# A planner whose lock between VectorE's and GpSimd's copies is more exact and covers Q copies too

## The chip, the cores and the metric

One core of a Trainium2 chip. The rounds of the experiments ran on three different chips, each with the kernel before alongside (714.64, 714.82 and 714.95 us). The metric is the device time of one execution in microseconds (us). The profile describes one execution; its span (first to last instruction) is 1.5 to 2.2 us shorter than the time in the runs on record. The granted TensorE clock was 1.00, within 0.003, in every profiled run here.

## The reference, cut to what matters

```python
def reference(A_x, A_wqkv, A_wo, B_x, B_w_gate, B_w_up, B_w_down, gate_w):   # S=2048, D=512
    x = A_x
    g = sigmoid((x * gate_w).sum(-1, keepdims=True))
    # a: 32 heads of width 16, softmax(q k^T / 4) v, then @ wo
    # b: ((x @ w_gate) * (x @ w_up)) @ w_down, inner width 1376
    return g * a + (1 - g) * b
```

Most of the time (693 of 713 us of the span, below) goes to the exponentials of the attention: 32 heads x 2048 x 2048 scores. In tiles of 128 keys x 512 queries that is 32 x 16 x 4 = 2048 score tiles. The kernel takes them in 32 rounds ("heads" in the prediction), each of four heads and one block of 512 queries, so 64 tiles.

## The kernel before

The kernel's Python simulates the five engines with a table of durations, picks at each step what an engine does next, and so fixes the order of all instructions on every engine. Only that order and the semaphores reach the chip. Three kinds of work matter here. (PSUM and SBUF are the two on-chip memories in which the kernel places its tiles. psS, psX and psO, which TensorE's matmuls write here (`PE MATMUL psS<-QM,KE` on the page), are allocated in PSUM, and the kernel calls 512 columns of them a bank; the other tiles are in SBUF.)

- ScalarE turns two or three score tiles at a time from PSUM into probabilities (1524 of the 2048 tiles).
- VectorE evaluates the other 524 by an integer trick (an "eviction" from PSUM), and then VectorE or GpSimd make three shifted copies of each pair of tiles, SBUF to SBUF ("probability copies").
- When the queries of a head block change, VectorE makes two masked copies of Q, SBUF to SBUF as well ("Q copies"). TensorE needs them for the next scores.

An extract, with comments added; `...` stands for lines left out:

```python
        # f_q: after the projection, PSUM -> qtmp, then two masked copies
        ev_q[c, b, p] = add("dve", [e0, o_mask] + q_last.get((c - 1, b), []),
            lambda v, p=p: v.tensor_scalar(QM[:, p, b, :], qtmp[:], mask[:, p : p + 1], None, ALU.mult),
            0.22, prio=3.2)
        ...
        # try_copy: one probability copy, on VectorE or on GpSimd
        if eng == "dve":
            fn = lambda v: v.tensor_single_scalar(cell_ap(c, I16), cell_ap(src, I16), 32.0 * k, ALU.add)
            occ = DCP + 0.133 * n           # 0.341 us for two tiles
        else:
            fn = lambda g: g.tensor_scalar(cell_ap(c, I16), cell_ap(src, I16), 32.0 * k, 1.0, ALU.add, ALU.mult)
            occ = PCP + 0.435 * n           # 1.01 us for two tiles
        ...
        # gen_step: the lock between VectorE's and GpSimd's copies
        if eng == "pool" and t < lock["dve"]:
            clock[eng] = lock["dve"]        # in the plan GpSimd waits for a VectorE copy to end
            return True
        ...
                if eng == "pool" or lock["pool"] <= t:   # VectorE copies wait for GpSimd
                    c = try_copy(eng, t)
        ...
        if eng == "pool":
            lock["pool"] = clock["pool"]
```

The planner's lock covers probability copies. A Q copy goes through the last lines of `gen_step` as an ordinary VectorE task: it neither waits for GpSimd nor holds it in the plan.

On the chip they do hold each other up, by the trace of this kernel. A Q copy that is not held takes 344 ns (mean of 20). Others, each begun while a GpSimd instruction ran, last 492 to 1169 ns and end 145 to 150 ns after it. 40 two-tile probability copies on VectorE (418 ns in the median where no GpSimd instruction overlaps them) also begin while one runs and end 277 to 282 ns after it. That is what "held" means below. Evictions from PSUM are not: 685.7 ns in the mean where a GpSimd instruction overlaps them (440), 682.7 where none does (84). The other way round, 33 GpSimd copies that begin 155 to 175 ns after a two-tile VectorE copy began take 1.152 us in the median, against 1.043 where no VectorE copy overlaps them. What on the chip makes the copies wait is not shown.

The softmax here doesn't subtract the row's maximum and nothing guards it: scores larger than these inputs give would overflow.

Of the kernel before, what the change touches and what calls it, by code (L numbers as in the profile page):

```python
# [13 lines left out]
class _Op:  # L14
# [5 lines left out]
    def __init__(self, eng, fn, deps, stream, inc):  # L20
        self.eng = eng
        self.fn = fn
        self.deps = deps
        self.stream = stream
        self.inc = inc
        self.seq = 0
        self.count = 0
        self.waits = []
        self.needed = False
        self.know = None  # L30
# [82 lines left out]

class _Task:

    __slots__ = ("eng", "deps", "fn", "occ", "lat", "prio", "cb", "stream", "dma", "op", "start", "end", "alloc", "pre")

    def __init__(self, eng, deps, fn, occ, lat=None, prio=5, cb=None, stream=None, dma=False, alloc=None):
        self.eng = eng
        self.deps = [d for d in deps if d is not None]  # L120
        self.fn = fn
        self.occ = occ
        self.lat = occ + 0.13 if lat is None else lat
        self.prio = prio
        self.cb = cb
        self.stream = stream
        self.dma = dma
        self.op = None
        self.start = None
        self.end = None  # L130
        self.alloc = alloc
        self.pre = None


class _Cell:

    __slots__ = ("need", "readers")
# [59 lines left out]
def _build(nc, A_x, A_wqkv, A_wo, W_gate, W_up, W_down, gate_w, out):  # L197
# [37 lines left out]
    with ExitStack() as stack:  # L235
# [243 lines left out]
            return old  # L479

        PACK = 0.2135
        PLAT = 0.44
        SW = 0.11
        pe = {"mode": "c"}
# [119 lines left out]
        def f_q(c, b, pos):  # L604
            packs = [
                (
                    lambda bk, kt=kt: col(
                        bk.ap, wq[:, kt, b * 128 : (b + 1) * 128], xT[:, kt, c * 512 : (c + 1) * 512], kt == 0, kt == KD - 1
                    ),
                    PACK,  # L610
                    "c",
                )
                for kt in range(KD)
            ]

            def evac(bk, last):
                if QT and (c or b):
                    bk.need += 1
                    e0 = add(
                        "dve",  # L620
                        [last] + qt_last,
                        lambda v: v.tensor_single_scalar(qtmp[:], bk.ap, QS, ALU.mult),
                        0.6,
                        prio=2,
                        cb=lambda k: bk.readers.append(k),
                    )
                    qt_last.clear()
                    for p in range(2):
                        ev_q[c, b, p] = add(
                            "dve",  # L630
                            [e0, o_mask] + q_last.get((c - 1, b), []),
                            lambda v, p=p: v.tensor_scalar(QM[:, p, b, :], qtmp[:], mask[:, p : p + 1], None, ALU.mult),
                            0.22,
                            prio=3.2,
                        )
                        qt_last.append(ev_q[c, b, p])
                    return
                bk.need += 2
                for p in range(2):
                    ev_q[c, b, p] = add(  # L640
                        "dve",
                        [last, o_mask] + q_last.get((c - 1, b), []),
                        lambda v, p=p: v.tensor_scalar(QM[:, p, b, :], bk.ap, mask[:, p : p + 1], QS, ALU.mult, ALU.mult),
                        0.66,
                        prio=2,
                        cb=lambda k: bk.readers.append(k),
                    )

            def deps():
                if c and not q_done.get((c - 1, b)):  # L650
                    return [None]
                return [d_wq[b]] + xdep(c)

            return Fill(f"q{c}{b}", packs, deps, evac, pos)
# [445 lines left out]
        def try_copy(eng, t):  # L1100
            best = None
            if eng == "pool" and dve_busy(t) < PB:
                return None
            for i, pr in enumerate(pairs):
                if not pr["k"] or not full(pr):
                    continue
                r = max(k.end for k in pr["p1"]) + (0.0 if eng == "dve" else SEM)
                if r > t:
                    continue
                if eng == "pool":  # L1110
                    k = pr["k"][-1]
                    if k < PK:
                        continue
                else:
                    k = pr["k"][0]
                    if k == 3 and r + (0.5 if st["ua"] >= NA - 12 else KW) > t:
                        continue
                best = (pr, k)
                break
            if best is None:  # L1120
                return None
            pr, k = best
            prs_ = [pr]
            if eng == "dve" and M4 and len(pr["u"]) == 2:
                for p2 in pairs[i + 1 : i + 4]:
                    if k in p2["k"] and full(p2) and len(p2["u"]) == 2 and max(x.end for x in p2["p1"]) <= t:
                        if even(pr["cell"] + p2["cell"]):
                            c = alloc(4, t)
                            if c is not None:
                                prs_.append(p2)  # L1130
                                break
            us = [(p_, x) for p_ in prs_ for x in range(len(p_["u"]))]
            n = len(us)
            c = alloc(max(n, 2), t)
            if c is None:
                return None
            c = c[:n]
            old = claim(c, 1)
            for p_ in prs_:
                p_["k"].remove(k)  # L1140
                if not p_["k"]:
                    pairs.remove(p_)
            if n == 4:
                _build.m4 += 1

            def cb(tk):
                for i, (p_, x) in enumerate(us):
                    cells[p_["cell"][x]].readers.append(tk)
                    add_tile(*p_["u"][x], k, c[i], tk)

            I16 = mybir.dt.int16
            src = tuple(p_["cell"][x] for p_, x in us)
            if eng == "dve":
                fn = lambda v: v.tensor_single_scalar(cell_ap(c, I16), cell_ap(src, I16), 32.0 * k, ALU.add)  # L1154
                occ = DCP + 0.133 * n
            else:
                fn = lambda g: g.tensor_scalar(cell_ap(c, I16), cell_ap(src, I16), 32.0 * k, 1.0, ALU.add, ALU.mult)  # L1157
                occ = PCP + 0.435 * n
            return _Task(eng, [x for p_ in prs_ for x in p_["p1"]] + old, fn, occ, cb=cb)
# [301 lines left out]
        PCP = 0.14  # L1461
        DEV = 0.6
        RSV = 0.5
        NP = 8
        KP = 1
        FBL = 15
# [233 lines left out]
        def gen_step(eng):  # L1700
            t = clock[eng]
            best = None
            if eng == "pool" and t < lock["dve"]:
                clock[eng] = lock["dve"]
                return True
            for k in qs[eng]:
                if best is not None and k.prio >= best.prio:
                    continue
                r = ready(k)
                if r is not None and r <= t:  # L1710
                    if k.alloc is not None:
                        old = k.alloc(t)
                        if old is None:
                            WHY.append((t, "p1cell"))
                            continue
                        k.deps = k.deps + old
                        k.alloc = None
                    best = k
# [4 lines left out]
            if eng in ("dve", "pool") and (best is None or best.prio > CPR):  # L1723
                if eng == "pool" or lock["pool"] <= t:
                    c = try_copy(eng, t)
                    if c is not None:
                        if eng == "dve":
                            lock["op"] = lock["prev"]
                            lock["prev"] = c
                        elif lock["op"] is not None:  # L1730
                            c.deps.append(lock["op"])
                        run_task(c, t)
                        lock[eng] = clock[eng]
                        return True
            if best is None:
                return False
# [1 line left out]
            if eng == "pool" and lock["op"] is not None:  # L1738
                best.deps.append(lock["op"])
            run_task(best, t)  # L1740
            if eng == "dve":
                lock["prev"] = best
            if eng == "pool":
                lock["pool"] = clock["pool"]
            return True

        o_woz = add(
# [208 lines left out]
```

## Time and profile before

| | before |
|---|---|
| time, median | 714.72 us (3 runs), 714.83 with a fourth run |
| span of the profile | 713.1 us |
| busy: ScalarE, TensorE, VectorE, GpSimd | 699.1, 688.0, 643.2, 439.2 us |
| exponentials on ScalarE | 496 of two tiles, 177 of three, 1 of one |
| Q copies | 30, mean 515 ns, longest 1169 ns |

How to read it: I split the span into four parts. The *lead* runs to the start of the first exponential, the *closing chain* from the end of the last one. Between them lie the exponentials. A *gap* is where the end of an exponential comes 0.04 us or more later after the end of the one before than is normal for its size (0.49, 0.917 and 1.344 us for one, two and three tiles). For before: lead 9.13, exponentials 693.03, gaps 1.47, closing 9.46, together 713.09 us. The gaps are worked out from the single instructions of the trace. They show waiting that the busy share hides, since ScalarE's records overlap (a two-tile one lasts 1.36 us in the median, while the ends lie 0.917 us apart).

### The profile page before, as it was taken

The page shows a single profiled execution, that of the slowest core. Times are in us where ns is not written, and L with a number is a line of the kernel's source. Part 1 is how long each engine was busy: PE and PEld are TensorE (multiplying, and loading weights), DVE is VectorE, ACT ScalarE, POOL GpSimd, SP SyncE. Part 2 cuts the span into 40 slices and gives each one's busy share as a digit, 9 for nine tenths or more (in the row PEclk, how much of TensorE's full clock was granted, in tenths as well). Part 3 has the DMA queues.
Part 4 walks back from the last instruction along what each step waited for, and adds up shares of the span by engine and source line. Part 5 has one row for each costly group of instructions (what it writes and reads, how often), then busy time and mean ns, then how long its engine had stood idle before and what let it go on. Part 6 is the DMA issues. An engine that isn't in the chain of part 4 may idle for free. (4 is left out here: it accounts for less than half of the span.)

```text
span 713.1 us, 21304 instructions
## 1 busy us (share of the span) xinstructions
PE 688.0 (96%) x9115; PEld 188.2 (26%) x9115; DVE 643.2 (90%) x1229; ACT 699.1 (98%) x689; POOL 439.2 (62%) x463
## 2 busy tenths in 40 slices
PE   8999999999999999999999999999999999999997
PEld 3323232222222222222222222222222222222222
DVE  5999989999999888899988888999889988999887
ACT  6999999999999999999999999999999999999995
POOL 4648676565656566576577566655557676555682
PEclk9999999999999999999999999999999999999999
DMA  7700001000200001000000010000000000000001
GB/s 142 255 12 9 21 18 19 19 17 22 81 20 18 17 16 32 26 17 17 20 3 28 17 44 25 18 13 10 21 18 17 18 28 29 17 21 18 3 20 46
DMA packets 33055, 21.65 MB, mean 30 GB/s; under 512 B 20381, under 2 KB 27965, under 8 KB 32961
## 3 DMA queue, kind: packets, MB, share of 16 engines
q1 hardware_dynamic: 31632, 19.64, 9.2%
q8 instruction: 71, 1.16, 0.7%
q10 hardware_dynamic: 1328, 0.66, 0.4%
q14 instruction: 24, 0.19, 0.1%
HBM read 15.12 MB, written 2.36 MB: 25 GB/s over the span
## 5 line engine op out<-in xcount | busy, mean ns | idle before, releaser
L1689 ACT ACTIVATE PT<-psS 128x1024 bf16<-128x1024 f32 (+1 forms) x577 | 625.9, 1420 | 0.7 <-PE psS L488 0.6
L1157 POOL TENSOR_SCALAR PT<-PT 128x1024 int16<-128x1024 int16 x220 | 237.0, 1086 | 146.1 <-DVE PT L1154 38.9
L488 PE MATMUL psS<-QM,KE 32*128 32x512 bf16 x1968 | 255.2, 376 | 12.3 <-ACT PT L1689 6.6
L1076 DVE TENSOR_SCALAR PT<-psS 128x512 int16<-128x512 f32 x328 | 221.8, 685 | 23.9 <-PE psS L488 20.2
L1219 PE MATMUL psO<-PT,VS 128*18 128x512 bf16 x1709 | 227.7, 381 | 0.7 <-DVE oraw L1248 0.6
L1219 PE MATMUL psO<-PT,VD 128*18 128x512 bf16 x1231 | 192.3, 381 | 0.1
L1017 PEld LDWEIGHTS <-KE 32*128 32x128 bf16 x2048 | 63.1, 91 | 279.4 <-issue 166.4
L1154 DVE TENSOR_SCALAR PT<-PT 128x1024 int16<-128x1024 int16 (+1 forms) x232 | 101.4, 466 | 2.1 <-PE psO L1219 0.8
L1157 POOL TENSOR_SCALAR PT<-wv 128x1024 int16<-128x1024 int16 x57 | 61.0, 1078 | 40.9 <-DVE wv L1076 16.5
L1219 PEld LDWEIGHTS psO<-PT,VS 128*18 128x18 bf16 x1709 | 52.2, 88 | 59.8 <-issue 42.4
L1689 ACT ACTIVATE wv<-psS 128x1024 bf16<-128x1024 f32 (+1 forms) x47 | 60.3, 1311 | 0.0
L557 PE MATMUL psX<-wd,hT 128*32 128x512 bf16 (+1 forms) x704 | 59.0, 386 | 0.3 <-DVE wk L867 0.3
L1076 DVE TENSOR_SCALAR wv<-psS 128x512 int16<-128x512 f32 x76 | 51.8, 686 | 6.8 <-PE psS L488 6.3
L1219 PEld LDWEIGHTS psO<-PT,VD 128*18 128x18 bf16 x1231 | 45.3, 88 | 36.4 <-issue 22.9
L557 PE MATMUL psX<-xT,wu 128*32 128x512 bf16 x688 | 53.2, 383 | 1.0 <-DVE wv L1076 0.7
L557 PE MATMUL psX<-xT,wg 128*32 128x512 bf16 x688 | 52.5, 383 | 1.0 <-DVE PT L1076 0.7
L1219 PE MATMUL psO<-wv,VS 128*18 128x512 bf16 x182 | 49.9, 381 | 0.5 <-DVE oraw L1248 0.5
L1076 DVE TENSOR_SCALAR PT<-psX 128x512 int16<-128x512 f32 x58 | 39.8, 686 | 6.6 <-PE psS L488 6.4
L1689 ACT ACTIVATE wd<-psS 128x1024 bf16<-128x1024 f32 (+1 forms) x35 | 42.0, 1289 | 0.0
L1219 PE MATMUL psO<-wv,VD 128*18 128x512 bf16 x167 | 38.2, 381 | 0.0
L1157 POOL TENSOR_SCALAR wv<-PT 128x1024 int16<-128x1024 int16 x24 | 25.6, 1068 | 20.3 <-PE psO L1219 10.0
L830 DVE TENSOR_TENSOR hT<-psX,usb 128x512 bf16<-128x512 f32 (+1 forms) x44 | 30.0, 682 | 4.4 <-PE psX L557 4.3
(127 smaller groups left out, 704.0 us busy)
## 6 DMA issues: line engine op xcount, KB each, us to landing
rb<-rscr SPq DMA_DIRECT2D x31, 256.0 KB
out_dram<-ost SPq DMA_DIRECT2D x12, 128.0 KB, 1.7
wu<-in_B_w_up_dram SPq DMA_DIRECT2D x1, 1376.0 KB, 10.1
wg<-in_B_w_gate_dram SPq DMA_DIRECT2D x1, 1376.0 KB, 13.0
wd<-in_B_w_down_dram SPq DMA_DIRECT2D x1, 1280.0 KB, 6.1
OT<-OX SPq DMA_DIRECT2D x60, 16.0 KB, 1.8
wo<-in_A_wo_dram SPq DMA_DIRECT2D x1, 512.0 KB, 13.0
out_dram<-wk SPq DMA_DIRECT2D x4, 128.0 KB, 1.7
```

The source lines that it names most:

```text
L488: return e.add_instruction(mybir.InstMatmult(name=nc.get_next_instruction_name(), engine=mybir.EngineType.PE, ins=[e.lower_ap(rhs), e.lowe ...
L557: return e.matmul(out_ap[32 * q : 32 * q + w, :], lhs[:, 32 * q : 32 * q + w], rhs, start=s0, stop=s1, tile_position=(0, 32 * q), skip_gro ...
L830: lambda v: v.tensor_tensor(hT[0:w, f, :], bk.ap[0:w, :], usb[0:w, n % 2, :], ALU.mult),
L1017: r = e.ldweights(w, tile_position=pos)
L1076: lambda v: v.tensor_scalar(cell_ap(pr["cell"][i : i + 1], mybir.dt.int16), bk.ap, CB, 0.0, ALU.add, ALU.max),
L1154: fn = lambda v: v.tensor_single_scalar(cell_ap(c, I16), cell_ap(src, I16), 32.0 * k, ALU.add)
L1157: fn = lambda g: g.tensor_scalar(cell_ap(c, I16), cell_ap(src, I16), 32.0 * k, 1.0, ALU.add, ALU.mult)
L1219: r = e.matmul(psO[32 * j : 32 * j + VW, :], pv_stationary(m, kt, j, k), cell_ap((cell,)), start=s0, stop=s1, tile_position=(0, 32 * j), s ...
L1689: lambda a: a.activation(cell_ap(c), src, ACT.Exp, scale=LN2 / 128.0),
```

## The change

Its intent: plan Q copies at 0.26 us (the trace has 256 to 264 ns from the start of one that is not held to the next instruction's start) and put them under the lock too; let each side start somewhat before the other's planned end (0.07 us before that of a VectorE copy, 0.1 us before that of a GpSimd copy); let GpSimd hold back when a Q copy is due within 0.3 us; and keep SBUF cells in reserve for the round that is accumulated now. The diff is cut to the lines that matter:

```diff
+        QMC = 0.26
+        LKD = -0.07
+        LKP = 0.1
+        QMP = 3.2
+        QMW = 0.3
@@ f_q
-                            0.22,
-                            prio=3.2,
+                            QMC,
+                            prio=QMP,
+                            x4=True,
@@ try_copy
-            c = alloc(max(n, 2), t)
+            c = alloc(max(n, 2), t, False, RSC * sum(len(x["k"]) for x in pairs if x["u"][0][0] <= pvst["m"]) if pr["u"][0][0] > pvst["m"] else 0)
@@ gen_step
-            if eng == "pool" and t < lock["dve"]:
-                clock[eng] = lock["dve"]
+            if eng == "pool" and t < lock["dve"] + LKD:
+                clock[eng] = lock["dve"] + LKD
+                return True
+            if eng == "pool" and QMW and clock["dve"] <= t + QMW and any(k.x4 and (ready(k) or 1e9) <= t + QMW for k in qs["dve"]):
+                clock[eng] += 0.05
                 return True
...
+                    if k.x4 and lock["pool"] > t:
+                        continue
...
-                        lock[eng] = clock[eng]
+                        lock[eng] = clock[eng] - (LKP if eng == "pool" else 0.0)
...
-            if eng == "dve":
+            if eng == "pool":
+                lock["pool"] = clock["pool"] - LKP
+            elif eng == "dve":
+                if best.x4:
+                    lock["dve"] = clock["dve"]
+                    lock["op"] = lock["prev"]
                 lock["prev"] = best
-            if eng == "pool":
-                lock["pool"] = clock["pool"]
```

`RSC` is 1.0. `lock["op"]` makes the next GpSimd instruction wait, by a real semaphore, for the VectorE instruction just ahead of the copy that is to go first.

More of the change, by code (lines that the diff above doesn't have):

```diff
@@ L114, with __init__ @@
 class _Task:
-    __slots__ = ("eng", "deps", "fn", "occ", "lat", "prio", "cb", "stream", "dma", "op", "start", "end", "alloc", "pre")
-    def __init__(self, eng, deps, fn, occ, lat=None, prio=5, cb=None, stream=None, dma=False, alloc=None):
+    __slots__ = ("eng", "deps", "fn", "occ", "lat", "prio", "cb", "stream", "dma", "op", "start", "end", "alloc", "pre", "x4")
+    def __init__(self, eng, deps, fn, occ, lat=None, prio=5, cb=None, stream=None, dma=False, alloc=None, x4=False):
         self.eng = eng
@@ L132, in __init__ @@
         self.pre = None
+        self.x4 = x4
 class _Cell:
@@ L1463, in _build @@
         RSV = 0.5
+        RSC = 1.0
         NP = 8
```

## The prediction

> **What bounds the kernel now.** The kernel's Python is a planner: it simulates the five engines with a small table of durations, decides the order of every instruction on each engine, and emits that fixed order with semaphores. So the change adds no work to the chip; it changes the order that the planner finds. I therefore first ask which engine has any time to give back.
>
> I read the busy rows, then the groups:
>
> ```profile
> PE 688.0 (96%) x9115; PEld 188.2 (26%) x9115; DVE 643.2 (90%) x1229; ACT 699.1 (98%) x689; POOL 439.2 (62%) x463
> ...
> L1689 ACT ACTIVATE PT<-psS 128x1024 bf16<-128x1024 f32 (+1 forms) x577 | 625.9, 1420 | 0.7 <-PE psS L488 0.6
> ...
> L632 DVE TENSOR_SCALAR QM<-qtmp,mask 128x512 bf16<-128x512 bf16 x30 | 14.3, 515 | 0.1
> ```
>
> ScalarE (ACT) is busy 699.1 of 713.1 us, and in the exponentials (L1689) it sits idle only 0.7 us before those that write PT. GpSimd (POOL) has 38% free and VectorE (DVE) 10%. The bound is ScalarE's exponentials. From the list of single instructions I take their rate: ends of neighbours lie 0.917 us apart where the second covers two score tiles (496 such), 1.344 us where it covers three (177), and one covers a single tile (about 0.49). 496 x 0.917 + 177 x 1.344 + 0.49 = 693.2 us; from the start of the first (9.1 us) to the end of the last (703.6 us) it is 694.5 us. The rest is 9.1 us of lead-in and 9.5 us of closing chain. Tiles: 2 x 496 + 3 x 177 + 1 = 1524, exactly the planner's own share for ScalarE (29 heads x 48 + 3 x 44), so no VectorE tile was shifted to ScalarE (`convert`) that a better plan could give back.
>
> So all the waiting of the bound, over the whole run, is about **1.5 us**: eight places where the spacing exceeds its normal by 0.04 us or more: 0.16 us at 14.8, 0.16 at 84.3, 0.10 at 130.3, 0.05 at 139.3, 0.09 at 143.9, 0.08 at 238.0, 0.32 at 313.7 and 0.52 at 450.2. Now the worst of them in the timelines of the three engines:
>
> ```profile
> 446.76 1.63 DVE L632 TENSOR_SCALAR QM<-qtmp,mask 128x512 bf16<-128x512 bf16 x2
> ...
> 446.16 2.08 POOL L1157 TENSOR_SCALAR PT<-PT 128x1024 int16<-128x1024 int16 x2
> ...
> 450.23 1.45 ACT L1689 ACTIVATE PT<-psS 128x1536 bf16<-128x1536 f32 x1 [0.41 <-PE psS L488]
> ```
>
> Two Q copies (QM<-qtmp) fill 1.63 us of VectorE while two GpSimd copies run. The next eviction from PSUM comes late, TensorE's timeline then shows a gap of 0.73 us released by that VectorE line, and ScalarE starves 3 us after the Q copies. The Q copies' own view shows it is a hold and not their length:
>
> ```profile
> L632 DVE TENSOR_SCALAR QM<-qtmp,mask x30: 336/346/1169, 38.1 to 569.0; 128x512 bf16<-128x512 bf16 x30
> ```
>
> Minimum, median, maximum: 336, 346 and 1169 ns. I listed all 30: 20 take 336 to 367 ns with no hold, 10 take 492 to 1169 ns, each begun while a GpSimd instruction ran and each ending 145 to 150 ns after it ended. Their excess over 344 ns sums to 30 x 0.515 - 30 x 0.344 = **5.1 us** of VectorE.
>
> [...] in the other direction a GpSimd copy takes 1.04 us alone but 1.15 us when it begins 0.17 us after a VectorE copy began. [...] The trace has 344, and 260 ns from one Q copy's start to the next start.
>
> **The change, part by part.** Nothing is removed from or added to the chip's work: 1229 DVE, 689 ACT and 463 POOL instructions stay nearly the same; only how copies divide between VectorE and GpSimd may move.
>
> 1. Q copies planned at 0.26 in place of 0.22 us[...]. 0.26 is what the trace shows start to start. They wait in the plan until GpSimd's lock ends, while VectorE does evictions instead, and GpSimd holds back when a Q copy is due within 0.3 us. Of the 5.1 us of holds I expect 4 to 5 to go. VectorE has 70 us idle, so none of this is on the path by itself. On the path is only what the holds cost ScalarE. Waits that follow a Q hold within 8 us: 0.16 (hold at 80.2), 0.05 + 0.09 (136.0), 0.32 (310.6), 0.52 (447.3), together **1.1 us**. The other six holds cost ScalarE nothing. I count 80% as saved: -0.9 us.
>
> 2. The lock's edges, -0.07 and -0.1 us. Both agree with the trace: a held probability copy ends 279 ns after GpSimd where an unheld one lasts 418, so it could be issued 0.14 us before GpSimd's recorded end, and that record (1.043) is 0.035 longer than GpSimd's back-to-back spacing (1.008): 0.10 remains. For GpSimd the lock ends 0.28 us after the VectorE copy's start, 0.06 before the planned 0.341. This buys about 0.1 us at each exchange, on engines with slack: no direct effect. Some 40 of 402 two-tile probability copies last over 440 ns, with 11 us of excess in all; the plan knew that lock, so I expect 5 to 12 us of it to stay.
>
> 3. GpSimd's holding back: 15 pairs of Q copies, up to 0.5 us each, under 8 us out of 274 us idle. Free.
>
> 4. The new reserve of cells for copies that belong to a later head (RSC): it delays such copies so that the head now being accumulated gets cells first. No exponential waits for cells in this trace, so I expect nothing, with some risk of later VectorE tiles.
>
> 5. A new order also changes how often ScalarE takes three tiles at once. Two triples for three pairs saves 3 x 0.917 - 2 x 1.344 = 0.06 us. Ten more triples are 0.3 us. I give this and the other small waits -0.3 us, since the constants were evidently tuned.
>
> Sum: 714.7 - 0.9 - 0.3 = **713.5 us**.
>
> **Rivals.** (a) Every hold is hidden, and the starvations at 313.7 and 450.2 come from TensorE's bank choice around a Q projection and return elsewhere: ScalarE's 98% and the six harmless holds speak for it, the chain Q copy, eviction, TensorE gap, ScalarE gap against it. Then 714.7, give or take 0.7. (b) The reserve and the strict waiting delay VectorE tiles, the planner's lag passes its limit of 6 and `convert` sends tiles to ScalarE: 0.43 us per tile (the step from 0.917 to 1.344). For it: the lag rule is a cliff; against: it fired zero times before and VectorE gains time. Five tiles would give 716. (c) VectorE was a hidden bound, and freeing 5 us there frees 5 us at the end: 709.6. Against it: VectorE's idle time exceeds that many times over and ScalarE has 1.5 us of waiting to give, so I reject it. A gain of over 2% can't happen: even with all 1524 tiles in triples, 508 x 1.344 = 682.8 us, plus 9.1 and 9.5, is 701.4 against 713.1, which is 1.6%.
>
> **Range and chances.** The lower end, 712.4: all 1.5 us of waiting goes and 25 triples more are found (0.8 us). The upper end, 715.2: the reordering makes a new starvation as large as the one at 450.2. Repeats of the old kernel lie within 0.43 us, so noise adds little. Faster by over 2%: 0.01; within 2%: 0.975; slower: 0.015, for a plan that goes badly wrong in reality.
>
> **What would show each step.** Right: the Q copies' maximum falls from 1169 to under 500 ns and their mean from 515 to about 350; VectorE's busy time falls by some 4 us; ScalarE's gaps at a Q copy vanish while its busy time stays within 1.5 us; the first exponential still starts at 9.1 us and the closing chain still takes about 9.5. Wrong: ScalarE tiles other than 1524, a ScalarE gap of over 0.5 us behind a GpSimd or cell wait, a triple count that moved by more than 30, or a closing chain that moved by more than 1 us.

The sum came to 714.7 - 0.9 - 0.3 = 713.5 us, with 0.9 for 80% (my estimate) of the 1.1 us of gaps behind held Q copies, and 0.3, an estimate too, for triples and small waits. The 344 and 260 ns are those of a Q copy that is not held; "in the other direction" speaks of the holds listed just before.

## The result, and the profile after

The changed kernel took 713.50 us (median of 4 runs, 713.11 to 713.63) against 714.83 us (714.56 to 714.99). The ratio is 0.9981 with a 95% interval of 0.9964 to 0.9998: faster by 0.2%. Ratios here are the mean time of one kernel's runs over that of the other's in the same rounds, so not quite the ratio of the medians that I quote.

Line numbers moved: L488, L632, L1076, L1154, L1157 and L1689 of before are L494, L638, L1083, L1161, L1164 and L1697 after. The busy row and the exponentials' group of the page after, and the Q copies' group from the list of groups by shape (busy us, mean ns of one, idle before):

```profile
PE 683.9 (96%) x9115; PEld 189.4 (27%) x9115; DVE 646.8 (91%) x1231; ACT 698.3 (98%) x683; POOL 455.2 (64%) x474
...
L1697 ACT ACTIVATE PT<-psS 128x1024 bf16<-128x1024 f32 (+1 forms) x562 | 619.6, 1462 | 0.2 <-PE psS L494 0.2
...
L638 DVE TENSOR_SCALAR QM<-qtmp,mask 128x512 bf16<-128x512 bf16 x30 | 10.8, 386 | 0.0
```

The Q copies' own view of the changed kernel; the last two lines say who waited for these copies, for how many us and how often:

```profile
L638 DVE TENSOR_SCALAR QM<-qtmp,mask x30: 255/346/745, 41.1 to 559.0; 128x512 bf16<-128x512 bf16 x30
...
  POOL PT L1164: 3.8, 7
  PEld L1024: 3.1, 6
```

The mean Q copy fell from 515 to 386 ns and the longest from 1169 to 745. GpSimd now is the one that waits: 3.8 us in 7 places ahead of copies into PT and, in lines of that view not shown, 1.2 us in two others. Before, no GpSimd instruction waited for a Q copy. ScalarE's idle time ahead of the exponentials that write PT went from 0.7 to 0.2 us. VectorE's busy time did not fall but rose, from 643.2 to 646.8.

By the four parts:

| us | before | after | difference |
|---|---|---|---|
| lead | 9.13 | 8.91 | -0.22 |
| exponentials (two / three tiles at once) | 693.03 (496 / 177) | 692.66 (480 / 188) | -0.37 |
| gaps | 1.47 | 0.53 | -0.94 |
| closing chain | 9.46 | 9.20 | -0.26 |
| span | 713.09 | 711.29 | -1.80 |

Both take 1524 tiles on ScalarE. The lead isn't the change's: another profile of the same changed kernel has 8.50. So noise of some 0.4 us lies in this row. The gaps of that other profile are 0.62, so here noise is some 0.1 us.

### The profile page after: what moved, and what is told of

The parts are those of the page before. It is cut to its first block, busy times and chain, and to the rows that moved or that the text cites. A ratio compares the mean times of both kernels' runs of the same rounds, so it can differ in the third digit from the quotient of the medians.

```text
span 711.3 us, 21337 instructions
## 1 busy us (share of the span) xinstructions
PE 683.9 (96%) x9115; PEld 189.4 (27%) x9115; DVE 646.8 (91%) x1231; ACT 698.3 (98%) x683; POOL 455.2 (64%) x474
## 3 DMA queue, kind: packets, MB, share of 16 engines
q8 instruction: 71, 1.16, 0.7%
## 5 line engine op out<-in xcount | busy, mean ns | idle before, releaser
L1697 ACT ACTIVATE PT<-psS 128x1024 bf16<-128x1024 f32 (+1 forms) x562 | 619.6, 1462 | 0.2 <-PE psS L494 0.2
L1164 POOL TENSOR_SCALAR PT<-PT 128x1024 int16<-128x1024 int16 x234 | 254.9, 1098 | 146.7 <-DVE PT L1083 56.7
L494 PE MATMUL psS<-QM,KE 32*128 32x512 bf16 x1969 | 253.1, 376 | 16.6 <-ACT PT L1697 9.7
L1083 DVE TENSOR_SCALAR PT<-psS 128x512 int16<-128x512 f32 x344 | 233.3, 686 | 26.6 <-PE psS L494 22.7
L1161 DVE TENSOR_SCALAR PT<-PT 128x1024 int16<-128x1024 int16 x242 | 107.4, 468 | 2.1
L1697 ACT ACTIVATE wv<-psS 128x1024 bf16<-128x1024 f32 (+1 forms) x52 | 71.2, 1378 | 0.0
L1164 POOL TENSOR_SCALAR PT<-wv 128x1024 int16<-128x1024 int16 x43 | 46.4, 1087 | 28.0 <-DVE wv L1083 8.9
L1697 ACT ACTIVATE wd<-psS 128x1024 bf16<-128x1024 f32 (+1 forms) x37 | 47.3, 1396 | 0.0
L1083 DVE TENSOR_SCALAR PT<-psX 128x512 int16<-128x512 f32 x62 | 42.6, 687 | 4.5 <-PE psS L494 3.5
L1083 DVE TENSOR_SCALAR wv<-psS 128x512 int16<-128x512 f32 x60 | 40.8, 687 | 5.4 <-PE psS L494 4.9
L1164 POOL TENSOR_SCALAR wv<-PT 128x1024 int16<-128x1024 int16 x29 | 30.5, 1052 | 22.6 <-PE psO L1226 8.4
L494 PE MATMUL psX<-QM,KE 32*128 32x512 bf16 x79 | 29.9, 378 | 3.3 <-ACT PT L1697 1.4
```

Of the source, the lines that this page charges most:

```text
L494: return e.add_instruction(mybir.InstMatmult(name=nc.get_next_instruction_name(), engine=mybir.EngineType.PE, ins=[e.lower_ap(rhs), e.lowe ...
L1083: lambda v: v.tensor_scalar(cell_ap(pr["cell"][i : i + 1], mybir.dt.int16), bk.ap, CB, 0.0, ALU.add, ALU.max),
L1697: lambda a: a.activation(cell_ap(c), src, ACT.Exp, scale=LN2 / 128.0),
```

## The experiments

**Theory H**: what a held Q copy takes from VectorE delays the next eviction, that delays TensorE's next use of the bank, and ScalarE starves. **Rival R**: the gain is the luck of another order (more triples, a shorter closing chain). **Rival E**: the tighter edges of the lock make the gain.

### 1. The old order, with the holds taken out

No engine's order changes; the traces of both kernels show the same sequence on every engine. Eight GpSimd instructions, which the trace of before shows holding a Q copy, are made to wait for the second Q copy of that pair (the diff is shortened):

```diff
+        for pi, qi in ((60, 3), (79, 5), (134, 9), (157, 11), (229, 17), (312, 23), (332, 25), (350, 27)):
+            o, q = pl[pi].op, qc[qi].op      # GpSimd instruction, Q copy
+            o.deps.append(q)                 # and listed after q, so that its wait can be placed
         P.emit(nc, stack)
```

> The kernel before with every engine's order unchanged; only eight GpSimd instructions, those that the trace of before shows holding a Q copy, are made to wait for that Q copy. Theory H (the holds of the Q copies starve ScalarE): the ScalarE gaps at 84, 139 to 144, 314 and 450 us (1.1 us in all) go, the span of the exponentials falls from 694.5 to about 693.4, time 713.6 to 714.0, a ratio near 0.9985; Q copies mean about 350 ns. Rival R (the gain of the change is only a luckier order: triples, closing chain): the gaps come back elsewhere and the time stays within 0.3 us of the 714.8 of before.

Measured: 714.17 us (5 runs, 714.00 to 714.50) against 714.64 (9 runs, 714.47 to 715.00), ratio 0.9993 (0.9980 to 1.0005). The time alone doesn't settle it; the trace says more. The Q copies' view:

```profile
L632 DVE TENSOR_SCALAR QM<-qtmp,mask x30: 336/347/371, 38.1 to 568.6; 128x512 bf16<-128x512 bf16 x30
```

All holds are gone (mean 347 ns). Around 310 us, first the kernel before (VectorE, GpSimd, then ScalarE; start us, us, what):

```profile
310.38 1.43 DVE L632 TENSOR_SCALAR QM<-qtmp,mask 128x512 bf16<-128x512 bf16 x2
311.73 0.67 DVE L1076 TENSOR_SCALAR PT<-psX 128x512 int16<-128x512 f32 x1
...
310.62 1.04 POOL L1157 TENSOR_SCALAR wv<-wv 128x1024 int16<-128x1024 int16 x1 [0.80 <-DVE wv L1076]
...
313.65 1.45 ACT L1689 ACTIVATE PT<-psS 128x1536 bf16<-128x1536 f32 x1 [0.21 <-PE psS L488]
```

and the same place in this experiment:

```profile
310.37 0.61 DVE L632 TENSOR_SCALAR QM<-qtmp,mask 128x512 bf16<-128x512 bf16 x2
310.89 0.68 DVE L1076 TENSOR_SCALAR PT<-psX 128x512 int16<-128x512 f32 x1
...
311.13 1.05 POOL L1157 TENSOR_SCALAR wv<-wv 128x1024 int16<-128x1024 int16 x1 [1.32 <-DVE QM L632]
...
310.75 4.94 ACT L1689 ACTIVATE PT<-psS 128x1024 bf16<-128x1024 f32 x4
```

GpSimd starts 0.5 us later, the eviction 0.84 us earlier, and ScalarE's gap at 314 us is gone: four exponentials follow one another. So are those at 84, 139 and 144. The gap at 450 shrank from 0.52 to 0.32 but another of 0.14 follows it, and two new ones (0.16 and 0.12) stand at 76.6 and 79.0 us. In all the gaps fell by 0.39 us, from 1.47 to 1.08, with lead, exponentials and closing chain alike to 0.01 us.

These four gaps, 0.73 us together, go back to the added waits, which delay GpSimd. At 450 us GpSimd's two copies start at 447.19 in place of 446.16. TensorE, which before had waited 0.73 us for the eviction, now waits for the first of them, and VectorE's four-tile probability copy is held by the second (1.05 us in place of 0.68):

```profile
448.30 0.39 PE L1219 MATMUL psO<-PT,VS 128*18 128x512 bf16 x2 [0.64 <-POOL PT L1157]
```

Behind the first added wait (GpSimd idle for 1.16 us at 62 us) GpSimd is still 0.63 us late at 73 us, and there it holds a VectorE probability copy. That copy before, then in this experiment with GpSimd's:

```profile
72.95 0.69 DVE L1154 TENSOR_SCALAR PT<-wd 128x1024 int16<-128x1024 int16 x1
...
72.97 1.30 DVE L1154 TENSOR_SCALAR PT<-wd 128x1024 int16<-128x1024 int16 x1
...
72.94 1.05 POOL L1157 TENSOR_SCALAR wd<-PT 128x1024 int16<-128x1024 int16 x1
```

VectorE's next evictions then come 0.6 us late, and the gaps at 76.6 and 79.0 follow. H is right in kind: a hold on VectorE does starve ScalarE. In size, all 1.13 us of gaps behind held Q copies are gone from the old order, and the edit's own price is 0.73 us: the net is 0.4 to 0.5 us, less than H expected and more than R.

### 2. The new order, with VectorE delayed at each pair of Q copies

The diff is cut by the lines that number VectorE's instructions anew:

```diff
+        for (qc, qb, qp), k in ev_q.items():
+            if k.x4 and qp == 0:
+                z = _Op("dve", lambda v, qb=qb: v.memset(QM[:, 0, qb, :], 1.0), list(k.op.deps), "dve", 1)
+                k.op.deps.append(z)
+                P.ops.insert(P.ops.index(k.op), z)
```

> The changed kernel with every engine's order kept; only VectorE gets one more instruction of some 0.6 us ahead of each of the 15 pairs of Q copies (a fill of the area that the Q copy then overwrites), in all about 9 to 10 us, twice the 5.1 us that the holds cost VectorE before. Theory H (what VectorE loses at a Q copy starves ScalarE): ScalarE gaps behind Q copies of 0.1 to 0.5 us each, in all 0.8 to 2 us, 714 to 715.5 us. Rival S (slack takes it, the gaps of before belonged to that order): gaps stay below 0.3 us more than in the changed kernel, 713.1 to 713.6 us.

Measured: 714.91 us (4 runs, 714.58 to 716.73). The ratio to before is 1.0010 (0.9993 to 1.0026). That is 1.4 to 1.8 us more than the changed kernel had in other rounds (713.50 and 713.07). The 15 fills took 7.3 us of VectorE (485 ns each), somewhat less than the 0.6 us each that I had put down as an estimate. Lead, exponentials and closing chain stayed (8.70, 692.70, 9.20); the gaps rose from 0.53 to 1.83 us. The largest of the new ones, 0.38 us, in the timelines of VectorE, TensorE and ScalarE:

```profile
558.31 0.48 DVE L1945 MEMSET QM<- 128x512 bf16 x1
558.83 0.77 DVE L638 TENSOR_SCALAR QM<-qtmp,mask 128x512 bf16<-128x512 bf16 x1
559.53 0.67 DVE L1083 TENSOR_SCALAR wv<-psX 128x512 int16<-128x512 f32 x1
...
560.25 1.05 PE L563 MATMUL psX<-xT,wu 128*32 128x512 bf16 x16 [0.70 <-DVE wv L1083]
...
561.66 1.02 ACT L1697 ACTIVATE PT<-psS 128x1024 bf16<-128x1024 f32 x1 [0.27 <-PE psS L494]
```

and in the changed kernel without the fill:

```profile
557.57 0.35 DVE L638 TENSOR_SCALAR QM<-qtmp,mask 128x512 bf16<-128x512 bf16 x1
557.83 0.68 DVE L1083 TENSOR_SCALAR wv<-psX 128x512 int16<-128x512 f32 x1
...
558.88 1.05 PE L563 MATMUL psX<-xT,wu 128*32 128x512 bf16 x16
...
556.73 6.31 ACT L1697 ACTIVATE PT<-psS 128x1536 bf16<-128x1536 f32 x5
```

This is the chain of the prediction, made on purpose: a late eviction of psX, 0.70 us of TensorE waiting for that bank to be free, and ScalarE dry soon after. I have followed this one gap only. The price is 1.30 / 7.3 = 0.18 us of gap per us of fill. The slack takes the rest. (The fill delays the Q copies too, for which TensorE waits 3.7 us in place of 3.1 and GpSimd's copies into PT 6.9 in place of 3.8, so not all of the price need be the evictions'. It also pushed this Q copy into a GpSimd copy that had begun meanwhile: 0.77 us in place of 0.35.) At that rate the 5.1 us of holds of before would be worth 0.9 us; experiment 1 found 0.4 net of its own price. Slack may well differ from order to order.

### 3. The parts of the change alone

Q copies as before, only the edges of the lock changed:

```diff
-        QMC = 0.26
+        QMC = 0.22
-                            x4=True,
+                            x4=False,
```

> The changed kernel with the Q copies planned as before (0.22 us[...]), so that only the two edges of the lock (-0.07 and -0.1 us) are left of the change. Theory H: Q copies are again held up to 1.1 us, with ScalarE gaps behind some of them, 714.5 to 717 us. Rival E (the tighter edges make the gain): 713.8 or less. Either way, if the tighter edges cause the longer holds of the probability copies seen in the changed kernel (19 us in place of 11), they are here too.

Measured: 717.21 us (5 runs, 716.84 to 717.66), ratio to before 1.0035 (1.0022 to 1.0047). Rival E falls: the edges alone make it slower. But H's reason does not hold here either. Q copies are held as much as ever (mean 538 ns, longest 1171, 5.8 us of excess), and yet the gaps are only 0.58 us. What is longer is the closing chain: 12.75 us against 9.46. The last eviction of a VectorE tile ends at 702.7 us, 0.5 us after the last exponential; in the changed kernel it ends 1.7 us ahead of it.

GpSimd's holding back taken out:

```diff
-        QMW = 0.3
+        QMW = 0.0
```

> The changed kernel without GpSimd's holding back (QMW = 0): Q copies wait in the plan for GpSimd's lock instead. If the holding back matters: Q copies come later by up to 1 us, VectorE fills the time with evictions; 714 to 715.5 us. If it does not matter: within 0.4 us of the changed kernel's 713.5. Q holds should stay under 0.75 us at most in both.

Measured: 713.79 us (5 runs, 713.64 to 714.93). In the same rounds the changed kernel took:

> The changed kernel once more in the same rounds as the three others: 713.5 us, ratio 0.998, to place them against it.

Measured: 713.07 us (5 runs, 712.74 to 713.54), ratio to before 0.9977 (0.9964 to 0.9989), which confirms the result. So the kernel without the holding back is 0.7 us slower, but not by Q copies: their mean is 360 ns, the longest 530, and none of its gaps follows a held one. Where the 0.7 us come from is not shown, since its profile fell on the slowest of its five runs (714.93). Against the changed kernel of these rounds that profile has 0.30 us more of exponentials (179 triples against 188), 0.42 more of closing chain (9.63 against 9.21), 0.99 more of gaps (the largest, 0.88 us at 22.5 us, ahead of all marked Q copies) and 0.64 more of lead.

Two more variants were built and not run. Without the cell reserve (`RSC = 0`) every engine's instruction list is the same as in the changed kernel, so this part does nothing here. With Q copies marked but the old edges (`LKD = LKP = 0`) the planner stops with an assertion: the simulated engines get stuck in the third block of queries. So "the Q part alone" can't be tried in this order. With the values 1 and 3 of experiment 4 it does build, but it was not run there.

### 4. Two other orders

Small changes of the planner reshuffle everything, so I changed the number that shuffles the places of the projections, in both kernels alike:

```diff
-        SEED = 2
+        SEED = 1     # and 3
```

> The kernel before with another value of the number that shuffles the fills' places (1 for 2), so another order from the same planner. It shows how much of the time is the luck of an order: the old value was evidently picked. 715 to 718 us, Q copies held up to 1.1 us, ScalarE gaps of 1 to 2.5 us.

> The changed kernel with the same other value. If the change is worth something beyond the luck of one order it beats its partner by 1 to 3 us: 713.5 to 715.5 us, ScalarE gaps under 1 us, Q copies held at most 0.75 us. If only luck, the pair is in either order.

> The changed kernel with the Q copies planned as before and the same other value. Theory H: ScalarE gaps behind held Q copies, over 1 us in all, slower than its partner that knows the Q copies. Rival: as with the first value, gaps of 0.6 us or less in spite of holds of 1 us, and what differs is the closing chain.

> The kernel before with a third value of the shuffling number (3). The first two values gave 714.8 and 716.4 us. 715.5 to 719 us, Q copies held up to 1.1 us.

> The changed kernel with that third value. The first two values gave gains of 1.3 and 1.5 us over their partners. If the gain belongs to the change: 1 to 3 us under its partner again. If it is luck of the order: in either direction.

Measured (2 runs each for values 1 and 3; the excess is over 344 ns per Q copy; the last column counts gaps within 8 us after a Q copy that lasted over 440 ns):

| kernel, value | time | exponentials | gaps | closing | longest Q copy | excess of Q copies | gaps behind held Q copies |
|---|---|---|---|---|---|---|---|
| before, 2 | 714.83 | 693.03 | 1.47 | 9.46 | 1169 ns | 5.1 | 1.13 |
| after, 2 | 713.50 | 692.66 | 0.53 | 9.20 | 745 | 1.2 | 0 |
| edges only, 2 | 717.21 | 692.93 | 0.58 | 12.75 | 1171 | 5.8 | 0.18 |
| before, 1 | 716.42 | 692.93 | 2.47 | 10.47 | 1229 | 5.7 | 0.71 |
| after, 1 | 714.89 | 692.90 | 0.87 | 10.12 | 747 | 1.1 | 0 |
| edges only, 1 | 716.77 | 692.87 | 2.11 | 11.74 | 1149 | 2.9 | 0 |
| before, 3 | 718.03 | 693.27 | 2.34 | 11.59 | 1360 | 9.0 | 1.95 |
| after, 3 | 714.28 | 692.55 | 0.86 | 9.71 | 740 | 0.5 | 0 |

The changed kernel wins all three pairs, by 1.33, 1.53 and 3.75 us. R has become unlikely as the sole cause, though three orders are few. Three things repeat in all pairs: no gap is left behind a held Q copy, the gaps fall by 0.9 to 1.6 us, and the longest Q copy falls to 0.75 us. (The zeros of the last column say little alone: the changed kernels have only 5, 3 and 2 Q copies over 440 ns, and the edges alone at value 1 have ten with no gap behind them. A hold costs ScalarE something in some places only.) The clearest hold of all is in the kernel before with value 3, VectorE and then ScalarE:

```profile
310.59 2.11 DVE L632 TENSOR_SCALAR QM<-qtmp,mask 128x512 bf16<-128x512 bf16 x2
312.62 0.68 DVE L1076 TENSOR_SCALAR wv<-psS 128x512 int16<-128x512 f32 x1
...
314.37 2.36 ACT L1689 ACTIVATE PT<-psS 128x1024 bf16<-128x1024 f32 x2 [0.68 <-PE psS L488]
```

But part of each difference is luck. Value 1 has the same 492 and 180 exponentials in both kernels, and its largest old gap (1.30 us at 543) has no Q copy within 20 us before it: an exponential waited there for a product of probabilities and values. Value 3 gains 1.88 us in the closing chain and 0.72 by triples (169 to 193). The edges without the Q part have a long closing chain in both orders tried (12.75 and 11.74). No Q copy begins after 584 us in any of these profiles, so its holds can't be what delays the end directly. Why the end comes out worse without them stays open.

### 5. A version that beats both

The gaps are now small, and ScalarE's exponentials remain the bound while VectorE is 9% free. So I gave VectorE four tiles of one more round, and picked an order out of some hundreds that the changed planner finds, by its own reckoning of the end:

```diff
-    HBQ = [16, 24, 30]
+    HBQ = [16, 22, 24, 30]      # second variant: [8, 16, 24, 30]
-        SEED = 2
+        SEED = 35                   # second variant: 9
```

> The changed kernel with four score tiles of one more head (22) evaluated on VectorE in place of ScalarE, and an order picked for it (shuffling number 35). ScalarE gives up four tiles of some 0.43 us: 1.7 us less exponential time, minus about 0.3 for fewer triples; VectorE and TensorE take 4 evictions, 12 copies and 12 products of probabilities and values more. 711.5 to 713 us against the changed kernel's 713.1 to 713.5. If VectorE or the cells were the bound now, 714 or more.

> The same with head 8 in place of head 22 and the shuffling number 9: 711.5 to 713 us by the same sum; if one of the two is above 714 the gain of such a shift hangs on the order found.

Measured: 711.23 us (4 runs, 710.89 to 711.54), ratio to before 0.9950 (0.9933 to 0.9966), and 711.80 us (4 runs, 711.57 to 712.18), ratio 0.9958 (0.9944 to 0.9973). Both give correct results. The busy row of the first:

```profile
PE 685.2 (97%) x9127; PEld 189.4 (27%) x9127; DVE 645.6 (91%) x1218; ACT 696.8 (98%) x685; POOL 476.8 (67%) x496
```

ScalarE takes 1520 tiles, its exponentials 691.06 us (1.6 less than in the changed kernel), and the gaps are 0.48 us. GpSimd takes most of the additional copies: 476.8 us in place of 455.2. The 1.6 us of exponentials belong to the four tiles. What the picked order adds is not separated, and the old planner was not given the same tiles and the same search.

## Why the prediction was right or wrong

The total was right: 713.5 us predicted, 713.50 measured. To 0.01 us that is luck: the span fell by 1.80 us where the terms said 1.2. The terms fared differently.

- **The bound and the size of what could be gained** were right. ScalarE stayed at 98%, its tiles at 1524, and the planner never shifted a tile to it (rival b). The 1.5 us of waiting was the pool that the gain had to come from; 0.94 of it went.
- **Step 1, Q copies (-0.9 us).** All gaps behind held Q copies (1.13 us) vanished, with small new ones elsewhere, for -0.94. So rival (a), by which they would return elsewhere, was wrong for this pair. But the same holds taken out of the old order brought only -0.39, since the waits that did it cost 0.73 of their own. How much of the 0.94 belongs to the holds and how much to the new order is not separated. The signs that I named were met only in part: the longest Q copy is 745 ns and not under 500, the mean 386 and not 350, and 3.9 of the 5.1 us of holds went, just under the 4 to 5 expected.
- **Readings that were off**, without harm to the sums: the list of before has 21 Q copies of 336 to 367 ns and 9 of 492 to 1169, so five and not six holds cost nothing.
- **Step 5, triples and small waits (-0.3 us).** Eleven more triples: -0.37 us. The closing chain gave another -0.26, which I had not counted. Within the span the sum is -1.80 with 0.22 of lead; in the time it is -1.33 by the medians and -1.41 by the profiled runs, since time less span was 1.79 us in the profiled run of before and 2.18 in that of after.
- **Step 2 failed: "I expect 5 to 12 us of it to stay", and with it "VectorE's busy time falls by some 4 us".** The excess of held two-tile probability copies rose from 11.5 to 19.3 us (40 to 77 copies over 440 ns), which outweighs the 3.9 us that the Q copies lost; VectorE's busy time rose by 3.6. With the edges alone it is the same, 20.7 us in 74 copies. So in this order it comes with the tighter edges and not with the marking of Q copies. At value 1 that is less clear: 17.1 us in 53 copies before, 17.9 in 67 with the edges alone and 22.6 in 82 with the whole change. (At value 3: 10.9 in 40 before, 22.0 in 82 after.) The reason is not shown. It cost nothing visible: the gaps are small in spite of it.
- **Step 3, "Free".** Not shown either way. GpSimd waits for Q copies for 5.0 us in 9 places, under the 8 that I allowed. Without the holding back the time is 0.7 us worse, and not by a held Q copy; by what is open (experiment 3).
- **Step 4**, the reserve: nothing, as predicted; the instruction lists are the same.
- **Rival (c)** is refuted: VectorE is busy for longer than before and the time fell.
- What the prediction hardly weighed ("the constants were evidently tuned"): value 2 is the best of the three tried, for both planners. With the two other values the old planner takes 1.6 and 3.2 us more, the new one 1.4 and 0.8.

## What to carry to other kernels

When a fixed order is planned from a table of durations, look in the trace for instructions whose longest time is far above their median: a resource may be missing from the plan. Then price it on the engine that bounds the kernel, by its gaps, and not by the time lost on the engine that was held: here 1 us of delay on VectorE cost ScalarE 0.1 (experiment 1, net: 0.39 of 5.1) to 0.2 us (experiment 2). Since any edit of a planner reshuffles everything, compare the old and the new one over several orders, or keep the order and change a single wait, and then look for what that wait itself delays.

## What the traces show at the edges of a hold

- By the profile's records (before) the two engines overlap at the edge of a hold: a two-tile VectorE copy that takes 418 ns alone ended 279 ns after the GpSimd copy that held it (median of 40), so some 0.14 us of it lies ahead of that record's end; and a GpSimd copy that began 0.25 us before the end of a VectorE copy took 1.15 us in place of 1.04 (33 of them), so it lost 0.11. Whether the hold ends earlier or the record runs on after it is not shown; of the 0.14, 0.035 is the excess of GpSimd's record (1.043) over its back-to-back spacing (1.008).
- The Q copies (512 elements a partition, times a scalar from `mask`) take 344 ns where they are not held, the two-tile probability copies (1024 elements, plus a constant) 418. Why half the elements take more than half the time is not shown.
- The next VectorE instruction starts 0.26 us after the start of a Q copy that is not held and 0.333 us after that of a two-tile probability copy (median of 162), some 80 ns before its recorded end. I would put these, and not the recorded durations, into a plan.
